# Local attention, channel mix and gated convolution on one core: six chunks of other widths, nine buffers for raw weights, another order

## The chip, the core and the metric

One Trainium2 chip, of which the program uses one core. TensorE (PE) multiplies, with its weight loads shown apart (PEld); VectorE (DVE), ScalarE (ACT) and GpSimd (POOL) do the rest; SyncE (SP) issues transfers. The metric is the time of one execution on the device in microseconds, the median of several runs.

## What is computed

Three steps on float32 data of 4 batches, 576 tokens and 512 channels (8 heads of 64), cut to what matters:

```python
# 1. attention in a window of +-3 tokens, plus attention on means of 4 tokens, repeated 4 times
q_d, k_d, v_d = (t.reshape(B, H, S // 4, 4, D).mean(axis=3) for t in (q, k, v))
out_up = np.repeat(sm_attn(q_d, k_d, v_d), 4, axis=2)
scores = np.where(np.abs(pos[:, None] - pos[None, :]) < 4, scale * q @ k.T, -1e9)
x = out_up + softmax(scores) @ v
# 2. channel mix
xk = mu_k * x + (1 - mu_k) * x_prev;  xr = mu_r * x + (1 - mu_r) * x_prev
v2 = np.maximum(xk @ w_k, 0.0) ** 2 @ w_v            # w_k 512 x 1024, w_v 1024 x 512
x1 = sigmoid(xr @ w_r) * v2                          # w_r 512 x 512
# 3. gated convolution over tokens
h = np.maximum(x1 @ w_in, 0.0)                       # w_in 512 x 1024
conv = sum(conv_w[k] * shifted(h, k - 1) for k in range(3))
out = (h * sigmoid(conv)) @ w_out                    # w_out 1024 x 512
```

## The kernel before

The program is recorded as steps. Each names an engine, a function that emits instructions, and the keys that it reads and writes. `Program.emit` emits the steps by a table of numbers, ORDER, written out in the file; a second table, SECOND, picks the second engine for steps that may run on either of two (`L435`/`L437`: a cast on ScalarE or VectorE). Each engine then works through its own instructions in that order, SyncE's queue of transfers too.

**Precision.** Weights arrive as 8-byte words (`st_d`, 128 partitions of 512 pairs, 512 KB a tile) and become float32 by two ScalarE instructions (`top` L396 into `st_f`, `cut` L415 in place) and one on VectorE (`bits` L399). For most products each operand is split into a high and a low part: a copy (`L435` or `L437`) and a subtraction (`L441`), and three matmuls (high x high, low x high, high x low) stand for one.

**Attention** (`group`, one group of four heads in a batch at a time): `pooled_kq` sums queries and keys by four on VectorE (L526); `local_scores` (L555 mask, L564) and `down_scores` (L629) are matmuls of 32 or 64 rows, followed by maxima, exponentials and normalisations on VectorE (L580 to L602, L646 to L673) and ScalarE (L593, L656, L671); `down_out` and `local_out` transpose the probabilities (L703, L759), copy them out of PSUM on ScalarE (L709, L764), and multiply by v (L727, L805). In batch 0 the means of v come from a matmul (`fold`, L499), and the first six of 18 query blocks are done by themselves, first.

**Channel mix**: `mix_prep` (L880, L888) builds xk for a chunk of tokens. The chunks are 192, 384 and four times 432 tokens. The first (`first_mix`, L919 and L949) multiplies by the raw float32 weights as they arrive, tile by tile (8 of w_k, 8 of w_v), while the tiles are being split for later. The others (`mix`) do 8 up products of 12 matmuls (L983), relu and square and split (L1002 to L1022, into the ring `k2` of 9 slots), and 4 down products of 24 (L1033). Attention of the following batches is placed between them. `out_of_mix` stores v2 to DRAM, `store_x` stores x.

**Last stage**: for five chunks of 384, 512, 512, 512 and 384 tokens, `load_chunk` reads x and v2 back, `gate` multiplies by w_r (L1324), `hidden` by w_in (L1372) with the convolution on VectorE (L1429 to L1442), and `outp` by w_out (L1467).

**What the change touches.** `floats` takes raw words from a ring of three tiles `st_d`: a load can be issued only when L399 has read the tile of three loads ago; until the first mix is done there are four tiles `st_f`. In memory, `first` holds what only the start needs; `mid` holds xk, k2 and the split w_r after it; `low` holds v2 of the last stage. `fills` (L1089) are 20 matmuls without use that stand between steps of the start. The factors mu are loaded by a transfer of their own (L1062) and completed by L1065.

Of the kernel before, what the change touches and what calls it, by code (L numbers as in the profile page):

```python
# [1569 lines left out]
```

## Time and profile before

| | |
|---|---|
| median of 3 runs | 556.81 us (555.5 to 561.09) |
| profiled execution | 556.9 us, its span 554.8 us |
| PE busy | 538.7 us, 97% of the span, 5364 matmuls |
| VectorE busy | 366.3 us, 66% |
| ScalarE busy | 300.3 us, 54% |
| GpSimd busy | 43.5 us, 8% |
| moved by DMA | 66.14 MB, mean 119 GB/s |
| chain that ended last | PE 91%, DMA 3%, DVE 3%, ACT 1%, issue 1% |

The span is counted from the first to the last instruction of the profiled execution. A share of busy time is a mean over stages: the first 77 us (attention of batch 0, the first chunk, the weights) are another kind of work than what follows.

### The profile page before, as it was taken

The numbers are of one execution on the slowest core, as the hardware profiler recorded it, in microseconds if no ns is written. First come the engines' busy times: TensorE is split into PE (matmuls) and PEld (weight loads), VectorE is DVE, ScalarE is ACT, GpSimd is POOL, SyncE is SP. The second block draws the span as 40 slices with busy tenths as digits, with TensorE's granted clock in tenths as the row PEclk, the third lists the DMA queues.
The fourth block names the chain that finished last, engine by engine and source line by source line (L and its number), as shares of the span: only waits on it lengthen the run. The fifth ranks groups of instructions, "written<-read, shape, count | busy, mean of one in ns | idle before, by whom it ended". The sixth has DMA issues, their size and how long they took to land.

```text
span 554.8 us, 12885 instructions
## 1 busy us (share of the span) xinstructions
PE 538.7 (97%) x5364; PEld 479.4 (86%) x5364; DVE 366.3 (66%) x689; ACT 300.3 (54%) x676; POOL 43.5 (8%) x181
## 2 busy tenths in 40 slices
PE   6899899999999999999999999999999999999996
PEld 3788789899898999999999998888888888899985
DVE  4699897675675385456366698579747867766750
ACT  2888676356556555464566646455535443442441
POOL 5001010110101000000000001002001101100000
PEclk9999999999999999999999999999999999999999
DMA  8577883477364614413616022232022000010021
GB/s 325 209 249 205 331 252 104 125 236 223 91 207 126 193 60 142 143 57 129 223 38 222 34 76 77 76 115 95 1 64 107 19 1 2 0 58 21 0 77 57
DMA packets 25402, 66.14 MB, mean 119 GB/s; under 512 B 2688, under 2 KB 8320, under 8 KB 24320
## 3 DMA queue, kind: packets, MB, share of 16 engines
q1 hardware_dynamic: 23616, 62.37, 32.5%
q0 software_dynamic: 1728, 2.95, 3.2%
q8 instruction: 42, 0.69, 0.5%
q14 instruction: 16, 0.13, 0.1%
HBM read 51.15 MB, written 14.16 MB: 118 GB/s over the span
## 4 chain that ended last, share of the span: by engine, by line
PE 91%; DMA 3%; DVE 3%; ACT 1%; issue 1%; SPq 0%; ACTq 0%; DVEq 0%
PE a L1467 18%; PE mm L983 17%; PE mm L1033 17%; PE mm L1372 9%; PE a L1372 9%; PE mm L1324 4%; PE a L1324 4%; PE a L805 3%; PE mm L919 2%; DMA st_d<-in_moe_w_v 2%; DMA vw<-in_vw 2%; PE a L703 1%; PE a L727 1%; PE a L564 1%; PE a L759 1%; PE a L629 1%
## 5 line engine op out<-in xcount | busy, mean ns | idle before, releaser
L983 PE MATMUL mm<-xk,wk 128*128 128x432 f32 (+1 forms) x480 | 97.0, 357 | 0.8 <-issue 0.8
L1033 PE MATMUL mm<-k,wv 128*128 128x432 f32 (+1 forms) x480 | 95.6, 356 | 0.0
L1033 PEld LDWEIGHTS mm<-k,wv 128*128 128x128 f32 x480 | 88.3, 188 | 3.9 <-issue 0.7
L983 PEld LDWEIGHTS mm<-xk,wk 128*128 128x128 f32 x480 | 88.0, 188 | 4.1 <-issue 1.1
L1467 PE MATMUL a<-wk,wv 128*128 128x512 f32 x342 | 81.0, 389 | 0.0
L1467 PEld LDWEIGHTS a<-wk,wv 128*128 128x128 f32 x342 | 64.2, 188 | 13.3
L1372 PE MATMUL mm<-k,wi 128*128 128x512 f32 (+2 forms) x240 | 52.0, 368 | 0.0
L1372 PE MATMUL a<-k,wi 128*128 128x512 f32 (+2 forms) x240 | 51.9, 368 | 0.0
L1372 PEld LDWEIGHTS mm<-k,wi 128*128 128x128 f32 x240 | 44.0, 188 | 5.8
L1372 PEld LDWEIGHTS a<-k,wi 128*128 128x128 f32 x240 | 43.9, 188 | 5.6
L1439 ACT ACTIVATE tmp<-tmp 128x513 f32<-128x513 f32 (+1 forms) x40 | 23.6, 592 | 36.3 <-DVE tmp L1433 36.1
L1002 ACT ACTIVATE tmp<-mm 128x432 f32<-128x432 f32 (+1 forms) x40 | 20.8, 522 | 26.1 <-PE mm L983 11.8
L399 DVE SCALAR_TENSOR_TENSOR st_f<-st_f,st_d 128x512 uint32<-128x512 uint32 x28 | 19.3, 689 | 23.1 <-ACT st_d L415 23.1
L1442 DVE SCALAR_TENSOR_TENSOR tmp<-tmp,h 128x384 f32<-128x384 f32 (+3 forms) x64 | 26.9, 456 | 7.2 <-ACT tmp L1439 5.8
L1022 DVE TENSOR_TENSOR k<-tmp,k 128x432 fp32r<-128x432 f32 (+1 forms) x40 | 23.5, 595 | 9.9 <-ACT k L1014 8.8
L1433 DVE SCALAR_TENSOR_TENSOR tmp<-h,cw_sb,tmp 128x513 f32<-128x513 f32 (+1 forms) x40 | 28.0, 700 | 1.8
L1430 DVE SCALAR_TENSOR_TENSOR tmp<-h,cw_sb,tmp 128x513 f32<-128x513 f32 (+1 forms) x40 | 28.0, 700 | 1.8
L1453 DVE TENSOR_TENSOR wv<-tmp,wv 128x512 fp32r<-128x512 f32 (+1 forms) x32 | 20.0, 628 | 11.6 <-ACT wv L1451 11.4
L391 POOL DMA_DIRECT2D vd<-in_vp x18 | 14.7, 817 | 162.1 <-DMA vd<-in_vp 96.9
L1429 DVE TENSOR_SCALAR tmp<-h,cw_sb 128x513 f32<-128x513 f32 (+1 forms) x40 | 18.4, 460 | 12.2 <-ACT h L1409 11.3
L1482 ACT ACTIVATE st_d<-a 128x512 f32<-128x512 f32 x18 | 10.5, 595 | 27.4 <-PE a L1467 23.7
L1451 ACT CAST wv<-tmp 128x512 fp32r<-128x512 f32 (+1 forms) x32 | 17.9, 571 | 11.8 <-DVE tmp L1442 11.6
(174 smaller groups left out, 874.8 us busy)
## 6 DMA issues: line engine op xcount, KB each, us to landing
vw<-in_vw SPq DMA_DIRECT2D x7, 1152.0 KB, 6.5
kq<-in_kq SPq DMA_DIRECT2D x6, 1152.0 KB, 6.4
x_d<-xT SPq DMA_DIRECT2D x16, 288.0 KB, 3.4
out_dram<-st_d SPq DMA_DIRECT2D x18, 256.0 KB, 2.1
st_d<-in_moe_w_k SPq DMA_DIRECT2D x8, 512.0 KB, 4.3
...
```

The source lines that it names most:

```text
L983: nc.tensor.matmul(pst[:, 0:n], lhsT=wk_t[wt][:, kt, mt * P:(mt + 1) * P], rhs=late["xk"][:, xs, kt, 0:n], start=(kt == 0 and g == 0), sto ...
L1002: lambda r=r, pst=pst: nc.scalar.activation(r, pst[:, 0:n], AF.Relu), (), [pk, rk],
L1022: lambda e, r=r, j=j: e.tensor_sub(late["k2"][1][:, j, 0:n], r, late["k2"][0][:, j, 0:n].bitcast(F32)),
L1033: nc.tensor.matmul(pst[:, 0:n], lhsT=wv_t[wt][:, kt, mt * P:(mt + 1) * P], rhs=late["k2"][xs][:, at[kt], 0:n], start=(kt == 0 and g == 0), ...
L1324: nc.tensor.matmul(pst[:, 0:n], lhsT=late["wr"][wt][:, kt, mt * P:(mt + 1) * P], rhs=r_t(c, xs, kt)[:, 0:n], start=(kt == 0 and g == 0), s ...
L1372: nc.tensor.matmul(pst[:, 0:n], lhsT=late["wi"][wt][:, kt, mt * P:(mt + 1) * P], rhs=x1s(xs, kt)[:, 0:n], start=(kt == 0 and g == 0), stop ...
L1430: nc.vector.scalar_tensor_tensor(out=cv, in0=tap(0), scalar=cw[:, 0, mt:mt + 1], in1=cv, op0=ALU.mult, op1=ALU.add)
L1433: nc.vector.scalar_tensor_tensor(out=cv, in0=tap(2), scalar=cw[:, 2, mt:mt + 1], in1=cv, op0=ALU.mult, op1=ALU.add)
L1439: step("ACT", act(m), lambda: nc.scalar.activation(cv, cv, AF.Tanh, scale=0.5), (), [cvk])
L1442: nc.vector.scalar_tensor_tensor(out=gf[:, o:q], in0=cv[:, o + j:q + j], scalar=1.0, in1=tap(1)[:, o + j:q + j], op0=ALU.add, op1=ALU.mult,)
L1453: ("DVE",), (dve(m),), lambda e: e.tensor_sub(gh_t(1, j)[:, 0:m], gf, gh_t(0, j)[:, 0:m].bitcast(F32)),
L1467: nc.tensor.matmul(pst, lhsT=xs[:, tt * P:(tt + 1) * P], rhs=wo[wt][:, kt, :], start=(kt == 0 and g == 0), stop=(kt == KF - 1 and g == 2),)
```

## The change

- The chunks of the channel mix are 192, 384, 512, 512, 384 and 320 tokens in place of 192, 384 and four of 432. `tmp` and xk grow to 512 columns, `k2` has 8 slots in place of 9.
- Six more tiles of raw words, `st_dd`, lie in `first`: the first nine weight tiles go to nine buffers, later ones to the three of before. The four `st_f` are used by the first twelve.
- The factors mu stand behind v's words in the rows of the first load of v (16 words more); a copy takes them from there. The load of mu is gone.
- Copies from PSUM in batch 0's attention, and the scaling of the first chunk's input, may run on VectorE or ScalarE. `copy` and `any_step` are new.
- The split w_r moves out of `mid` to a pool of its own that takes the place of `sq`; v2 of the last stage lies in `tmp`, one of two tiles of the convolution in the last pool.
- ORDER and SECOND are new tables.

```diff
 ORDER = [
-    4, 3, 79, 8, 9, 5, 10, 201, 0, 81, 69, 13, 70, 66, 2, 61, 62, 80, 15, 16, 97, 23, 17, 89, 24, 25, 63, 26,
+    3, 4, 9, 8, 5, 10, 96, 0, 80, 65, 14, 78, 66, 68, 1, 104, 15, 16, 200, 2, 17, 22, 18, 64, 63, 88, 23, 69,
...
-    NT = 3 * S // 4
+    NT = 4 * P
     ROW = -(-NT // 64) * 64
-    chunks_ = [(0, NH), (NH, S - NH)] + [(t, NT) for t in range(S, B * S, NT)]
-    K2 = 9
+    sizes = [NH, S - NH, NT, NT, 3 * P]
+    sizes.append(B * S - sum(sizes))
+    chunks_ = [(sum(sizes[:i]), n) for i, n in enumerate(sizes)]
+    K2 = 8
...
-    vw_t = several(att, 1, [P, NB // 2, 4, D], F32, "vw") + several(first, 1, [P, NB // 2, 4, D], F32, "vw_f")
+    VW = NB // 2 * 4 * D
+    vw_m = att.tile([P, VW + 16], F32, name="vw")
+    vw_t = [vw_m[:, 0:VW].rearrange("p (e h d) -> p e h d", h=4, d=D)] + several(first, 1, [P, NB // 2, 4, D], F32, "vw_f")
...
+    st_d += several(first, 6, [P, 512, 2], U32, "st_dd")
...
-    def ring(name, tiles, one=0):
+    def ring(name, tiles, one=0, until=None):
         i = count[name] = count.get(name, -1) + 1
-        i %= one or len(tiles)
+        i %= one if until is not None and i >= until else len(tiles) if until is not None else one or len(tiles)
         return tiles[i], (name, i)
...
-        d, dk = ring("st_d", st_d)
+        d, dk = ring("st_d", st_d, 3, 9)
...
-        f, fk = ring("st_f", st_f, 2 * bool(late))
+        f, fk = ring("st_f", st_f, 2, 12)
...
+        def copy(eng, o, i):
+            if eng is nc.vector:
+                eng.tensor_copy(o, i)
+            else:
+                nc.scalar.copy(o, i)
+
+        def any_step(n, f, r, w, slack):
+            if b == 0:
+                step(("ACT", "DVE"), (act(n), 0.12 + 1.0e-3 * n), f, r, w, slack=slack)
+            else:
+                step("ACT", act(n), lambda: f(nc.scalar), r, w, slack=slack)
...
-            load(t.rearrange("p e h d -> p (e h d)"), vw[b, gp], NB // 2 * 4 * D, (), [k], SL[0])
+            if b == 0 and gp == 0:
+                load(vw_m, vw[b, gp], VW + 16, (), [k, "mus0"], SL[0])
+            else:
+                load(t.rearrange("p e h d -> p (e h d)"), vw[b, gp, :, 0:VW], VW, (), [k], SL[0])
...
-                def cp(a=a, e=e, pst=pst):
-                    nc.scalar.copy(pt[:, a:e].rearrange("p i r -> p (i r)"), pst[:, 0:(e - a) * P])
-                step("ACT", act((e - a) * P), cp, (), pks + [(ptk, a)], slack=SL[i0 > 0])
+                def cp(eng, a=a, e=e, pst=pst):
+                    copy(eng, pt[:, a:e].rearrange("p i r -> p (i r)"), pst[:, 0:(e - a) * P])
+                any_step((e - a) * P, cp, (), pks + [(ptk, a)], SL[i0 > 0])
...
-    step("SP", 0.2, lambda: nc.sync.dma_start(out=mus[:, 0:2], in_=mu), (), ["mus0"])
-    step(
-        "DVE", 0.17,
-        lambda: nc.vector.tensor_scalar(mus[:, 2:4], mus[:, 0:2], -1.0, 1.0, op0=ALU.mult, op1=ALU.add),
-        ["mus0"], ["mus"],
-    )
+    def factors():
+        nc.vector.tensor_copy(mus[:, 0:2].rearrange("p a k -> p (a k)"), vw_m[:, VW:VW + 2 * KM])
+        nc.vector.tensor_scalar(mus[:, 2:4], mus[:, 0:2], -1.0, 1.0, op0=ALU.mult, op1=ALU.add)
+
+    step("DVE", 0.28, factors, ["mus0"], ["mus"])
...
-        late["wr"] = several(mid, 2, [P, KM, DM], F32R, "wr")
...
+    def open_wr():
+        sq_pool.release()
+        late["wrp"] = wrp = tc.alloc_tile_pool(name="wrp", bufs=1, reuse_waits="tile")
+        late["wr"] = several(wrp, 2, [P, KM, DM], F32R, "wr")
...
     def v_t(i, kt):
-        return cutout(st_d[1 + kt // 2], kt % 2 * CH, CH, F32) if i else late["v"][0][:, kt]
+        return cutout(st_d[1 + kt // 2], kt % 2 * CH, CH, F32) if i else tmp[:, kt]
...
+    def cv_t(i):
+        return cutout(tmp, KM * NT + 2 * CH, CH + 1, F32) if i else late["cv"][0]
```

Two places of the new order. The first is SyncE's queue, from the second group's queries and keys on. `kq` and `vw` are queries with keys, and v's rows; `kq_f` and `vw_f` those of the second group; `st_d` and `st_dd` are tiles of raw weight words. Before:

```order
L383 DMA kq_f_127<-in_kq 128x768 x2
L383 DMA vw_130<-in_vw 128x2304
L383 DMA vw_f_131<-in_vw 128x2304
L409 DMA st_d_110<-in_moe_w_k 128x1024
L1062 DMA mus<-in_mu 128x8
L383 DMA kq_f_127<-in_kq 128x2x384
L409 DMA st_d_112<-in_moe_w_k 128x1024
L409 DMA st_d_111<-in_moe_w_k 128x1024
L409 DMA st_d_110<-in_moe_w_k 128x1024
L409 DMA st_d_111<-in_moe_w_k 128x1024
```

Now, from the same load on:

```order
L389 DMA kq_f_127<-in_kq 128x768 x2
L389 DMA vw<-in_vw 128x2320
L389 DMA vw_f_131<-in_vw 128x2304
L415 DMA st_d_112<-in_moe_w_k 128x1024
L415 DMA st_d_110<-in_moe_w_k 128x1024
L389 DMA kq_126<-in_kq 128x2x384
L415 DMA st_dd_148<-in_moe_w_k 128x1024
L415 DMA st_d_111<-in_moe_w_k 128x1024
L415 DMA st_dd_150<-in_moe_w_k 128x1024
L389 DMA kq_f_127<-in_kq 128x2x384
L415 DMA st_d_110<-in_moe_w_v 128x1024
L415 DMA st_dd_151<-in_moe_w_k 128x1024
```

The rest of the first group's queries and keys (`kq_126`, 384 columns of two pairs), which stood ahead of these rows, now stands behind two tiles of w_k; five tiles of w_k go out ahead of the first load that reuses a tile (`st_d_110` for w_v), where it was three; the load of mu is gone.

The second place is VectorE's work from the first raw weights to the first channel-mix matmul's inputs. `st_f`, `st_ff` are float32 tiles of w_k, `wk_115` and `wk_116` their high and low parts, `tmp<-xT,mus` the mixed input, one row for each of four tiles of 128 channels. Before:

```order
L399 SCALAR_TENSOR_TENSOR st_f_113<-st_f_113,st_d_110 128x512
L399 SCALAR_TENSOR_TENSOR st_f_114<-st_f_114,st_d_111 128x512
L437 CAST wk_115<-st_f_114 128x4x128
L441 TENSOR_TENSOR wk_116<-st_f_114,wk_115 128x4x128
L888 SCALAR_TENSOR_TENSOR tmp<-xT_119,mus,tmp 128x192
L399 SCALAR_TENSOR_TENSOR st_ff_146<-st_ff_146,st_d_112 128x512
L888 SCALAR_TENSOR_TENSOR tmp<-xT_119,mus,tmp 128x192
L441 TENSOR_TENSOR wk_116<-st_f_113,wk_115 128x4x128
L888 SCALAR_TENSOR_TENSOR tmp<-xT_119,mus,tmp 128x192 x2
```

Now:

```order
L901 TENSOR_SCALAR tmp<-xT_119,mus 128x192
L916 SCALAR_TENSOR_TENSOR tmp<-xT_119,mus,tmp 128x192
L443 CAST wk_115<-st_ff_146 128x4x128
L405 SCALAR_TENSOR_TENSOR st_f_113<-st_f_113,st_d_110 128x512
L447 TENSOR_TENSOR wk_116<-st_ff_146,wk_115 128x4x128
L443 CAST wk_115<-st_f_113 128x4x128
L916 SCALAR_TENSOR_TENSOR tmp<-xT_119,mus,tmp 128x192 x2
L405 SCALAR_TENSOR_TENSOR st_ff_147<-st_ff_147,st_dd_148 128x512
L447 TENSOR_TENSOR wk_116<-st_f_113,wk_115 128x4x128
L916 SCALAR_TENSOR_TENSOR tmp<-xT_119,mus,tmp 128x192
```

One tile's bits (`st_ff_146`) stand just ahead of these rows. The first input's scaling has come over from ScalarE (L901), a second cast too, and the third tile's bits stand between the last two inputs.

## Rows read from the trace of the kernel before

**Rows 1.** The page's head and its first part: busy us, share of span, instructions.

```profile
span 554.8 us, 12885 instructions
PE 538.7 (97%) x5364; PEld 479.4 (86%) x5364; DVE 366.3 (66%) x689; ACT 300.3 (54%) x676; POOL 43.5 (8%) x181
```

**Rows 2.** Busy time by stage; the first row names the columns.

```profile
core 0: us, PE busy (x) PEld busy (x) DVE busy (x) ACT busy (x) POOL busy (x), PEclk, DMA share, GB/s
0.00:4.85 4.85, 0.86 (x4) 0.59 (x5) 0.06 (x1) 2.34 (x5) 3.74 (x20) 1.00 0.61 202
4.85:20.80 15.95, 14.66 (x311) 9.35 (x310) 10.84 (x30) 6.19 (x20) 4.48 (x22) 1.00 0.86 335
18.00:23.00 5.00, 4.66 (x157) 4.34 (x155) 2.18 (x6) 4.26 (x11) 0.00 (x0) 1.00 0.17 49
20.80:28.40 7.60, 6.13 (x242) 5.17 (x239) 4.97 (x12) 7.18 (x16) 0.00 (x0) 0.89 0.49 157
28.40:77.80 49.40, 45.21 (x1059) 40.73 (x1060) 45.37 (x93) 39.07 (x99) 4.17 (x5) 0.98 0.78 258
77.80:131.00 53.20, 52.40 (x870) 48.77 (x869) 36.92 (x70) 31.74 (x85) 5.65 (x7) 1.00 0.61 185
131.00:304.00 173.00, 173.00 (x1736) 162.38 (x1736) 98.32 (x185) 96.41 (x210) 5.55 (x15) 1.00 0.42 136
304.00:551.00 247.00, 246.46 (x1153) 212.37 (x1151) 169.80 (x304) 116.69 (x240) 19.94 (x113) 1.00 0.15 49
```

**Rows 3.** The chain that ended last, in order of time: start us, us, what.

```profile
3.15 8.67 DMA vw<-in_vw
...
59.06 9.62 DMA st_d<-in_moe_w_v
...
77.03 3.34 PE mm L983 x18
...
100.99 2.08 PE mm L1033 x12
...
210.12 18.80 PE mm L1033 x96
...
389.41 21.76 PE a L1467 x96
```

**Rows 4.** SyncE's waits, 0 to 80 us: total us, times, longest.

```profile
SPq L409 <- DVE st_f L399: 22.7, 8, 5.6
SPq L409 <- DVE st_ff L399: 13.8, 6, 4.7
```

**Rows 5.** Waits of PE (4 to 30 us), VectorE and ScalarE (28.4 to 77.8 us).

```profile
PE mm L499 <- DMA vw<-in_vw: 1.3, 1, 1.3
...
DVE st_ff L399 <- ACT st_d L415: 1.0, 1, 1.0
DVE kqd L526 <- DMA kq<-in_kq: 0.8, 1, 0.8
DVE st_f L399 <- ACT st_d L415: 0.5, 2, 0.3
...
ACT st_ff L396 <- DMA st_d<-in_moe_w_v: 2.3, 2, 1.6
...
ACT st_f L396 <- DMA st_d<-in_moe_w_v: 0.9, 1, 0.9
```

**Rows 6.** Groups by line and form: xcount, busy us, mean ns, idle before.

```profile
L581 DVE TENSOR_TENSOR probs<-a,sums 128x684 f32<-128x684 f32 x6 | 5.2, 871 | 0.2
L673 DVE TENSOR_TENSOR pd<-pd,sums 128x720 f32<-128x720 f32 x4 | 3.6, 904 | 0.1
L437 DVE CAST wk<-st_f 128x512 fp32r<-128x512 f32 x5 | 2.1, 423 | 0.1
L888 DVE SCALAR_TENSOR_TENSOR tmp<-xT,mus,tmp 128x192 f32<-128x192 f32 x4 | 1.6, 413 | 0.0
L824 DVE COPY xT<-a 128x192 f32<-128x192 f32 x2 | 0.7, 359 | 1.3 <-PE a L805 1.3
...
L671 ACT ACTIVATE pd<-pd,sums 128x144 f32<-128x144 f32 x13 | 4.3, 406 | 2.7 <-DVE sums L536 2.6
```

**Rows 7.** Instructions in order of time, VectorE and PE: start us, us, what.

```profile
27.73 0.74 DVE L888 SCALAR_TENSOR_TENSOR tmp<-xT,mus,tmp 128x192 f32<-128x192 f32 x2
28.25 2.52 PE L919 MATMUL mm<-tmp,st_f 128*128 128x192 f32 x8
...
34.97 1.50 PE L919 MATMUL mm<-tmp,st_ff 128*128 128x192 f32 x8
```

More of the change, by code (lines that the diff above doesn't have):

```diff
@@ L380, in tile_local_attention__then__channel_mix__then__conv_glu, with load @@
     step("POOL", 4.7, make_picks, (), ["picks"])
-    def load(o, i, words, r, w, slack=1.0, rows=P):
-        step("SP", dma_us(words, rows), lambda: nc.sync.dma_start(out=o, in_=i), r, w, slack=slack)
+    def load(o, i, words, r, w, slack=1.0, rows=P, k=1.0):
+        step("SP", k * dma_us(words, rows), lambda: nc.sync.dma_start(out=o, in_=i), r, w, slack=slack)
     def load_sum(o, planes, words, keys, slack, rows=P):
@@ L471, in loads @@
                     len(prs) * (e - a), (),
-                    [(k, i, pr) for pr in prs for i in ({0, half} if whole else {i0})], SL[i0 > 0],
+                    [(k, i, pr) for pr in prs for i in ({0, half} if whole else {i0})], SL[i0 > 0], P, 1.0,
                 )
@@ L736, in down_out, with cp @@
             whole = m // BQ * BQ
-            def cp():
-                nc.scalar.copy(od[:, :, 0:whole], po[:, :, 0:whole])
+            def cp(eng):
+                copy(eng, od[:, :, 0:whole], po[:, :, 0:whole])
                 if m > whole:
-                    nc.scalar.copy(od[:, :, whole:m], po[:, :, nq * BQ - (m - whole):nq * BQ])
-            step("ACT", act(2 * whole), cp, (), pks + [odk], slack=SL[i0 > 0])
+                    copy(eng, od[:, :, whole:m], po[:, :, nq * BQ - (m - whole):nq * BQ])
+            any_step(2 * whole, cp, (), pks + [odk], SL[i0 > 0])
         def local_out(i0, i1):
@@ L1110, in open_mid @@
         late["k2"] = several(mid, 2, [P, K2, ROW], F32R, "k2")
-        late["wr"] = several(mid, 2, [P, KM, DM], F32R, "wr")
-    seconds = [("st_f", 2), ("st_f", 3)] + [(x, 1) for x in ("kq", "kqd", "vw", "vd", "probs", "pd")]
+    seconds = [("st_f", 2), ("st_f", 3)] + [("st_d", 3 + i) for i in range(6)] + [(x, 1) for x in ("kq", "kqd", "vw", "vd", "probs", "pd")]
     step("", 0.0, open_mid, (), [k for k in prog.writer if root(k, seconds)] + ["mid"])
     late["two"] = True
-    by_columns(w_r, lambda: late["wr"][0], lambda: late["wr"][1], KM, range(KM), "wr", ["mid"])
+    def open_wr():
+        sq_pool.release()
+        late["wrp"] = wrp = tc.alloc_tile_pool(name="wrp", bufs=1, reuse_waits="tile")
+        late["wr"] = several(wrp, 2, [P, KM, DM], F32R, "wr")
+    step("", 0.0, open_wr, ["mid"], [k for k in prog.writer if root(k) == "sq"] + ["wrp"])
+    by_columns(w_r, lambda: late["wr"][0], lambda: late["wr"][1], KM, range(KM), "wr", ["wrp"])
     store_x(0)
@@ L1139, in tile_local_attention__then__channel_mix__then__conv_glu @@
     att_keys = [k for k in prog.writer if root(k) in names]
-    sq_keys = [k for k in prog.writer if root(k) == "sq"]
     def open_late():
-        sq_pool.release()
         att.release()
-        late["low"] = low = tc.alloc_tile_pool(name="low", bufs=1, reuse_waits="tile")
-        late["v"] = several(low, 1, [P, KM, CH], F32, "v")
         wb = late["pool"] = tc.alloc_tile_pool(name="wb", bufs=1, side="right", reuse_waits="tile")
@@ L1151, in open_late @@
         late["edge"] = several(wb, 1, [P, KF, ahead + 1], F32, "edge")
-        wb.tile([P, 72], F32, name="gap2")
-    step("", 0.0, open_late, (), att_keys + sq_keys + ["late"])
+        late["cv"] = several(wb, 1, [P, CH + 1], F32, "cv")
+        wb.tile([P, 192], F32, name="gap2")
+    step("", 0.0, open_late, ["wrp"], att_keys + ["late"])
     class Late:
@@ L1219, in v_dst @@
             return [(2 * j, 2 * j + 2, flat(st_d[1 + j], F32).rearrange("p (k c) -> p k c", k=2)) for j in range(2)]
-        return [(0, KM, late["v"][0])]
-    v_old = ("late", "st_old")
+        return [(0, KM, tmp[:, 0:KM])]
+    v_old = ("tmp_lo", "st_old")
     xrf = [cutout(xT[1], CH * i, CH, F32) for i in range(2)]
@@ L1225, in tile_local_attention__then__channel_mix__then__conv_glu @@
     os_t = [cutout(st_d[0], DM * i, DM, F32) for i in range(2)]
-    cv_t = [cutout(tmp, (CH + 1) * i, CH + 1, F32) for i in range(2)]
-    gt_t = [cutout(tmp, 2 * (CH + 1) + CH * i, CH, F32) for i in range(2)]
+    gt_t = [cutout(tmp, KM * NT + CH * i, CH, F32) for i in range(2)]
+    def cv_t(i):
+        return cutout(tmp, KM * NT + 2 * CH, CH + 1, F32) if i else late["cv"][0]
     GB = 10
@@ L1239, in tile_local_attention__then__channel_mix__then__conv_glu @@
     step("", 0.0, lambda: None, (), keys_of("k2") + ["k2_old"])
+    step("", 0.0, lambda: None, (), [k for k in prog.writer if k[0] == "tmp" and k[1] < KM] + ["tmp_lo"])
     step("", 0.0, lambda: None, (), keys_of("tmp") + ["tmp_old"])
@@ L1423, in hidden @@
         parts = [0] + [t - outs[c][0] for t in seam] + [m]
-        cv, cvk = ring("cv", cv_t)
+        ci, cvk = ring("cv", (0, 1))
         gt, gk = ring("gt", gt_t)
-        cv, gf = cv[:, 0:m + gap], gt[:, 0:m]
+        gf = gt[:, 0:m]
         def conv():
+            cv = cv_t(ci)[:, 0:m + gap]
             nc.vector.tensor_scalar_mul(cv, tap(1), cw[:, 1, mt:mt + 1])
@@ L1437, in hidden, with tanh @@
         hks = [(hk, "pad"), (hk, "d")]
-        step("DVE", 0.43 + 3.36e-3 * m, conv, hks + ["cw", "tmp_old"], [cvk])
-        step("ACT", act(m), lambda: nc.scalar.activation(cv, cv, AF.Tanh, scale=0.5), (), [cvk])
+        step("DVE", 0.43 + 3.36e-3 * m, conv, hks + ["cw", "tmp_old", "late"], [cvk])
+        def tanh():
+            cv = cv_t(ci)[:, 0:m + gap]
+            nc.scalar.activation(cv, cv, AF.Tanh, scale=0.5)
+        step("ACT", act(m), tanh, (), [cvk])
         def glu():
+            cv = cv_t(ci)
             for j, (o, q) in enumerate(zip(parts, parts[1:])):
@@ L1508, in tile_local_attention__then__channel_mix__then__conv_glu @@
     late["pool"].release()
-    late["low"].release()
+    late["wrp"].release()
     late["mid"].release()
@@ L1514 @@
 _INS = [
[L1515 removed]
+    "kq", "vp", "vw", "moe_w_k", "moe_w_v", "moe_w_r",
     "moe2_w_in", "moe2_conv_w", "moe2_w_out",
@@ L1546 @@
     laid["vp"] = vd.transpose(0, 1, 5, 6, 2, 4, 3, 7).reshape(B, H // 4, 80, FAC, -1)
-    laid["mu"] = np.stack([inputs[x].reshape(-1, P).T for x in ("moe_mu_k", "moe_mu_r")], axis=1)
+    mu = np.stack([inputs[x].reshape(-1, P).T for x in ("moe_mu_k", "moe_mu_r")], axis=1).reshape(P, -1)
+    vw = laid["vw"]
+    laid["vw"] = np.zeros((*vw.shape[:3], vw.shape[3] + 16), vw.dtype)
+    laid["vw"][..., :vw.shape[3]] = vw
+    laid["vw"][0, 0, :, vw.shape[3]:vw.shape[3] + mu.shape[1]] = mu
     laid["moe2_conv_w"] = inputs["moe2_conv_w"].reshape(3, -1, P).transpose(2, 0, 1).reshape(P, -1)
```

42 lines of the change are left out of this document (22 added, 20 removed), and 165 rows, old and new, of tables (ORDER, SECOND).

## The prediction

> **What bounds the kernel now.** I read the engines' busy times first. TensorE is busy for 538.7 of 554.8 us [rows 1], so only about 16 us of the span are without a matmul, and the other two ways to win time are cheaper matmuls and fewer fillers. The table by stage [rows 2] then shows where the 16 us lie. From 131 us to the end PE shows no gap but the store at the very end: 173.00 of 173.00 and 246.46 of 247.00. Between 77.8 and 131 it misses 0.8 us. The rest, 3.99 + 1.29 + 1.47 + 4.19 = 10.9 us, lies ahead of 77.8 us. In the columns beside them, the stretch from 28.4 to 77.8 has VectorE at 45.37 of 49.40 us; ScalarE has 39.07. So the kernel has two parts: a start of 77 us in which VectorE (and ScalarE close behind) feeds PE, and 477 us in which only the cost of the matmuls counts.
>
> The chain of waits, in order of time [rows 3], says the same. Ahead of 77 us it passes through transfers (v's rows to 11.8 us, a tile of w_v from 59.06 to 68.68 us) and then VectorE; behind that it is blocks of matmuls back to back. The sync engine's waits [rows 4] tell why the tile of w_v was late: its queue stood for 22.7 and 13.8 us at loads of raw weights, until VectorE's L399 had emptied one of three buffers. DMA meanwhile moved 49 GB/s from 18 to 23 us, against 335 GB/s in the stretch ahead [rows 2].
>
> **The change, part by part.** All sums are against the profiled execution, 554.8 us of span; its time was 556.9 us, so 2.1 us lie around the span, and the median of the runs shown (556.81) is the same time.
>
> *Chunks.* The number of chunks stays six, so the number of matmuls stays (192 in each chunk with split operands, 96 up and 96 down), and the columns sum to the same 2304. Only the price of a column changes. Blocks without a gap give it [rows 3]: 96 of 432 columns take 18.80 us, 195.8 ns each; 96 of 512 columns 21.76 us, 226.7 ns; 12 of 384 columns 2.08 us, 173.3 ns. Over 1/2.4 ns a column that is 15.8, 13.3 and 13.3 ns a matmul. A width of 320 does not occur. With the surplus of 384 and 512 it is 146.7 ns, with that of 432 it is 149.2; I take 146.7, since a line drawn through 384 and 512 down to 320 gives it too. Before: 4 x 192 x 195.8 = 150.4 us. After: 192 x (226.7 + 226.7 + 173.3 + 146.7) = 148.5 us. That is **-1.9 us**, or -1.4 at the other end. It falls in the part where PE has no gap, so all of it reaches the end, as long as what feeds PE keeps up: from 131 to 304 us VectorE is busy for 98.32 and ScalarE for 96.41 of 173 us [rows 2], so a block of 12 shorter by 0.6 us (146.7 against 195.8 ns) still leaves them room, and two blocks of down products stand between the last square of a chunk and the block that needs it.
>
> Against this speaks a rule of the Trainium skill, page "TensorE: Matmul & The Clock Gate", section "Wait — 56ns, not 53.3ns?": back to back, a warm matmul starts N / 2.4 GHz plus a fixed 2.5 ns after the one ahead of it. By that rule equal columns in equally many matmuls cost the same, and the sum would lack the 1.9 us. The trace does not agree with it: 15.8 ns at 432 and 13.3 ns at 512 columns [rows 3].
>
> *Nine raw-word buffers.* Six more tiles let the first nine loads of weights go without L399 having emptied one. In SP's order five loads of w_k now stand ahead of the first that must wait (before, three). The price of the waits that go: ScalarE stood 2.3 + 0.9 us for tiles of w_v, and VectorE 1.0 us behind that, and 0.8 us for queries and keys queued at SP behind such loads [rows 5]. VectorE bounds the stretch. Its idle time there is 49.4 - 45.4 = 4.0 us, its whole list of named waits 3.2 us. I count 1.0 + 0.8 + 0.5 (the two short waits for the cut of raw words) = **-2.3 us**; the bounds are 0 (another wait takes the place) and -4.0 (VectorE never stands).
>
> *Work that moves between VectorE and ScalarE.* Some evacuations of PSUM in batch 0 and the first scaling may now run on VectorE. By the order on both engines, from the start to the last piece of the first split chunk VectorE gets 138 instructions in place of 131: eleven come, four go. Nine of the new ones are copies from PSUM of 256 to 768 columns, which VectorE does not do in this trace. I price them along the line through its copy of 192 columns (359 ns) and its subtraction from PSUM of 684 (871 ns) [rows 6]: 0.43 us for each of five with 256, 0.56 for 384, 0.69 for each of two with 512, 0.96 for 768, in all 5.05 us. The scaling (at most 0.41, as L888 on 192 columns) and the copy of the factors (8 words, below 0.2) make it 5.6. What goes: two copies of 192 (0.72), a normalisation of 720 columns (0.904), a cast (0.423). Net +3.6 us. But it comes early: ahead of the first matmul of the channel mix VectorE is idle for 15.95 - 10.84 + 7.60 - 4.97 = 7.7 us [rows 2], which covers the 4.0 us that fall there. Behind it, in the stretch that counts, VectorE gets the copies of 768 and one of 256 columns and loses the normalisation and two casts: 0.96 + 0.43 - 0.90 - 0.85 = -0.4 us. I leave that at **0**, since ScalarE takes the normalisation in five pieces of 0.406 us [rows 6], though it has 49.40 - 39.07 = 10 us of room there. If the early cover were gone, the 4.0 us would be on the path.
>
> *Order at the start.* SP's second load is now the other half-batch's, and the rest of the first queries and keys (384 columns of two pairs, 0.39 MB, 1.2 us at 335 GB/s) comes behind v's rows. The first fold of v waited 1.3 us for those rows [rows 5], which landed at 3.15 + 8.67 = 11.82 us [rows 3]; it can start up to 1.2 us earlier. What follows is attention of the first six blocks on PE, VectorE and ScalarE in turn, up to L399 and L888, whose last piece ended at 27.73 + 0.74 = 28.47 us [rows 7]. That last piece stands behind three tiles' bits, as before, and now behind one cast more; so I take **-0.5 us** of the 1.2, bounds +1 and -1.2.
>
> *The rest.* The factors ride in v's rows: one small load fewer, one tiny copy more on VectorE (0.1 us, early): 0. Twenty fillers stay twenty. PE's granted clock is at 0.89 from 20.8 to 28.4 and at 0.98 from 28.4 to 77.8 us [rows 2], a stretch at 1.2 GHz after small waits around 25 us; the first channel-mix matmuls still wait for the same work, so I leave it as it is. The k2 ring of eight serves eight products: its slots 0 to 3 are read for the last time a block before the chunk's last. Where v, cv and the gate's tiles lie in the last stage adds no instruction; VectorE has 247 - 170 us of room there: 0, as is the new order of blocks. Switches between attention and mix number 29 in place of 28.
>
> **Sum**: 554.8 - 1.9 - 2.3 - 0.5 = 550.1 us of span, 552.2 us with the 2.1 around it.
>
> **Rivals.**
> 1. *VectorE never stands.* Its idle 4.0 us vanish, the start gains all 1.2 us, and the 0.8 us behind 77.8 too: 554.8 - 1.9 - 4.0 - 1.2 - 0.8 = 546.9, 549.0 us in all. For it: no load of raw words is on the path any more. Against: ScalarE has 2 us more there, and each tile passes ScalarE, VectorE, PE in turn.
> 2. *The buffers bring nothing.* VectorE was at 92% there; its waits for transfers turn into waits for ScalarE. Only the columns are left: 552.9, 555.0 us in all. For it: 45 us of VectorE's work stay.
> 3. *The width isn't it.* The 432's surplus comes from the stage's operands, not its width, and chunks of 512 pay it too, or all pay one floor: 550.1 + 1.9 = 552.0, 554.1 us in all. Against: L1033 at 384 columns, same operands, has 13.3 ns. The rule of the Trainium skill named above gives this time. The trace bears it out in nothing but the equal surplus of 384 and 512.
> 4. *Slower.* The copies given to VectorE come in its full stretch and not in the idle one ahead: the place is its queue between the folds of v and the first bits, the price 4.0 us, less the columns' 1.9: 556.9, 559.0 us in all. It decides once the first channel-mix matmul starts 2 us behind 28.25 us. Beyond it a second stretch at 1.2 GHz at the start would cost about what the first did (a block of 8 in 2.52 in place of 1.50 us [rows 7]).
>
> **How the numbers follow.** Forecast 0.52, rival 1 0.22, rival 2 0.14, rival 3 0.04, rival 4 0.08. The predicted time is the forecast's, 552.2 us. The range leaves out rival 4 (0.08) and the half of rival 1 that lies below its time (0.11): 549.0 to 556.0 us, which holds the ends of the column and buffer terms too. A measurement can tell about 1% from no change: faster is below 551.2, slower above 562.4. Faster: rival 1 and a sixth of the forecast, 0.31; slower: what of rival 4 reaches past 562.4, and the unseen, 0.07; same: the rest, 0.62.
>
> **What would show it.** Right: blocks of 96 in 21.76 us (512) and about 14.1 us (320); SP's waits at L399's successor much shorter until 50 us; no wait of ScalarE for w_v; the first product of 384 columns at about 74 us in place of 77.03; PE without gaps from 131 us on. Wrong: VectorE busy over 95% and the 384s no earlier (rival 2); 512 at more than 228 ns (rival 3); the first channel-mix matmul behind 30 us (rival 4); gaps on PE in the chunk of 320 columns or at the first gates.

## The result, and the profile after

The changed kernel takes 552.02 us (median of ten runs, 551.51 to 552.67), the kernel before beside it 556.62 us (ten runs, 555.31 to 561.09): a ratio of 0.990, interval 0.988 to 0.993. Run once more with the last experiments it took 551.84 us. So it is faster by 4.6 us, close to the forecast of 552.2 us; that is 0.8%, less than the 1% from which the prediction counted a change. The parts of the forecast fared less evenly than its sum.

The page's head and first part, to be read beside [rows 1]:

```profile
span 550.3 us, 12876 instructions
PE 537.8 (98%) x5364; PEld 469.2 (85%) x5364; DVE 376.6 (68%) x711; ACT 290.7 (53%) x655; POOL 47.0 (9%) x181
```

The number of matmuls is the same, TensorE's busy time fell by 0.9 us only, and the span by 4.5. Busy time by stage, with the columns of [rows 2]; the fourth row runs from the last piece of the first mix input to the first product of 384 columns:

```profile
4.85:20.80 15.95, 14.97 (x314) 9.85 (x312) 11.36 (x33) 4.99 (x16) 4.38 (x24) 1.00 0.99 391
18.00:23.00 5.00, 4.15 (x116) 3.71 (x110) 2.38 (x6) 1.59 (x4) 0.00 (x0) 0.91 0.64 249
20.80:28.40 7.60, 7.16 (x241) 6.09 (x238) 6.05 (x14) 4.90 (x12) 0.00 (x0) 0.59 0.20 60
29.14:74.83 45.69, 43.85 (x1056) 38.70 (x1054) 44.10 (x89) 39.88 (x104) 4.17 (x5) 1.00 0.70 229
131.00:299.47 168.47, 168.47 (x1804) 149.86 (x1803) 99.25 (x189) 86.29 (x190) 5.54 (x15) 1.00 0.41 129
```

The stretch of the fourth row in the kernel before:

```profile
28.47:77.03 48.56, 44.37 (x1055) 39.89 (x1055) 44.60 (x91) 38.96 (x99) 4.17 (x5) 0.98 0.77 257
```

VectorE's work in it hardly changed (44.60, then 44.10 us), but it stands for 45.69 - 44.10 = 1.6 us in place of 48.56 - 44.60 = 4.0 us. Ahead of it TensorE's granted clock is 0.59 from 20.8 to 28.4 us, where it was 0.89 [rows 2]. Where each stage begins, from the timeline of VectorE and TensorE (start us, us, what):

```profile
28.74 0.40 DVE L916 SCALAR_TENSOR_TENSOR tmp<-xT,mus,tmp 128x192 f32<-128x192 f32 x1
...
74.83 6.63 PE L1011 MATMUL mm<-xk,wk 128*128 128x384 f32 x36
...
125.05 1.31 PE L1011 MATMUL mm<-xk,wk 128*128 128x512 f32 x5
...
299.31 0.87 PE L1353 MATMUL mm<-xk,wr 128*128 128x386 f32 x4
```

With the same four places before (28.47, 76.95, 128.77 and 303.95 us by its timeline) the 4.5 us are:

| stretch | before | after | difference |
|---|---|---|---|
| to the last piece of the first mix input | 28.47 | 29.14 | +0.7 |
| from there to the first product of 384 columns | 48.48 | 45.69 | -2.8 |
| the chunk of 384 | 51.82 | 50.22 | -1.6 |
| the four wide chunks | 175.18 | 174.26 | -0.9 |
| last stage | 250.9 | 251.0 | +0.1 |

The chunk of 384 and the wide chunks share attention work: the new order puts 80 fewer local score matmuls, with 4 masks, into the chunk of 384 (by the matmuls' start times this work takes 1.97 us there in place of 3.05) and as many more behind it. Without that shift of about 1.1 us the chunk of 384 gained about 0.5 us and the wide chunks about 2.0 us. In a second profile of the changed kernel (span 549.5 us, the last of the experiments) the four places are at 29.17, 75.09, 124.07 and 298.36 us: the chunk of 384 takes 48.97 us there, 1.3 less than in the table, and the other stretches differ by 0.3 at most.

The 0.7 us to the last piece were lost ahead of ScalarE's and VectorE's work for it. By the chain these two take 7.4 us to that piece in both kernels, from the first of the next rows before and from the second now (start us, us, what):

```profile
21.08 0.58 ACT pdt L709
```

```profile
21.73 0.03 ACT xT L841
```

TensorE's wait for v's rows at the first fold (1.3 us before) is gone from the list of waits all the same. Which step of the attention ahead of 21.7 us became longer was not tested.

SyncE's waits to 80 us and the named waits of VectorE (28 to 76 us) and TensorE (74 to 300 us), beside [rows 4, 5]:

```profile
SPq L415 <- DVE st_f L405: 21.7, 3, 11.0
SPq L389 <- PE a L746: 11.7, 2, 6.4
SPq L415 <- DVE st_ff L405: 8.1, 2, 5.3
...
DVE pt L468 <- PE a L778: 0.6, 1, 0.6
DVE sums L556 <- ACT pd L677: 0.2, 1, 0.2
...
PE a L746 <- DMA vd<-in_vp: 0.9, 1, 0.9
```

SyncE's queue still stands for 21.7 + 8.1 us at loads of raw words, in five waits where there were fourteen; but nobody waits for w_v any more, and VectorE's named waits fell from 3.2 to 0.8 us. TensorE's wait of 0.9 us at 86.15 us is new.

### The profile page after: what moved, and what is told of

Same layout as the page of the kernel before. It is cut to its first block, busy times and chain, and to the rows that moved or that the text cites. A ratio compares the mean times of both kernels' runs of the same rounds, so it can differ in the third digit from the quotient of the medians.

```text
span 550.3 us, 12876 instructions
## 1 busy us (share of the span) xinstructions
PE 537.8 (98%) x5364; PEld 469.2 (85%) x5364; DVE 376.6 (68%) x711; ACT 290.7 (53%) x655; POOL 47.0 (9%) x181
## 4 chain that ended last, share of the span: by engine, by line
PE 90%; DMA 4%; DVE 2%; POOL 1%; ACT 1%; issue 1%; ACTq 0%; POOLq 0%
PE a L1504 18%; PE mm L1061 17%; PE mm L1011 15%; PE mm L1401 9%; PE a L1401 9%; PE mm L1353 5%; PE a L1353 4%; DMA vd<-in_vp 4%; PE a L824 3%; PE mm L947 2%; PE a L746 2%; PE a L724 1%; PE mm L977 1%; PE a L585 1%; PE a L778 1%; PE a L650 1%
## 5 line engine op out<-in xcount | busy, mean ns | idle before, releaser
L1061 PE MATMUL mm<-k,wv 128*128 128x384 f32 (+2 forms) x480 | 95.6, 355 | 0.0
L1011 PE MATMUL mm<-xk,wk 128*128 128x384 f32 (+2 forms) x480 | 95.5, 355 | 0.0
L1030 ACT ACTIVATE tmp<-mm 128x384 f32<-128x384 f32 (+2 forms) x40 | 20.8, 524 | 36.6 <-PE mm L1011 32.0
L1037 DVE TENSOR_TENSOR tmp<-tmp 128x512 f32<-128x512 f32 (+2 forms) x28 | 16.4, 591 | 24.0 <-ACT tmp L1030 24.0
L397 POOL DMA_DIRECT2D vd<-in_vp x18 | 14.7, 815 | 163.8 <-DMA vd<-in_vp 130.9
L1050 DVE TENSOR_TENSOR k<-tmp,k 128x384 fp32r<-128x384 f32 (+2 forms) x40 | 23.2, 592 | 7.9 <-ACT k L1042 7.2
L1353 PE MATMUL mm<-xk,wr 128*128 128x512 f32 (+2 forms) x120 | 26.1, 369 | 0.0
L1353 PE MATMUL a<-xk,wr 128*128 128x512 f32 (+2 forms) x120 | 25.9, 368 | 0.0
L1353 PEld LDWEIGHTS a<-xk,wr 128*128 128x128 f32 x120 | 22.0, 188 | 2.8
L1353 PEld LDWEIGHTS mm<-xk,wr 128*128 128x128 f32 x120 | 21.9, 188 | 2.8
L1504 PE MATMUL a<-wk,k 128*128 128x512 f32 x90 | 22.9, 390 | 0.0
```

What stands on the lines that cost most here:

```text
L397: lambda i=i: nc.gpsimd.dma_start(out=o, in_=i, accum_op=ALU.add), (), keys, slack=slack,
L1011: nc.tensor.matmul(pst[:, 0:n], lhsT=wk_t[wt][:, kt, mt * P:(mt + 1) * P], rhs=late["xk"][:, xs, kt, 0:n], start=(kt == 0 and g == 0), sto ...
L1030: lambda r=r, pst=pst: nc.scalar.activation(r, pst[:, 0:n], AF.Relu), (), [pk, rk],
L1037: e.tensor_tensor(out=r, in0=r, in1=r, op=ALU.mult)
L1050: lambda e, r=r, j=j: e.tensor_sub(late["k2"][1][:, j, 0:n], r, late["k2"][0][:, j, 0:n].bitcast(F32)),
L1061: nc.tensor.matmul(pst[:, 0:n], lhsT=wv_t[wt][:, kt, mt * P:(mt + 1) * P], rhs=late["k2"][xs][:, at[kt], 0:n], start=(kt == 0 and g == 0), ...
```

## The experiments

### The chunks' widths alone

```diff
-    sizes = [NH, S - NH, NT, NT, 3 * P]
-    sizes.append(B * S - sum(sizes))
+    sizes = [NH, S - NH] + [3 * S // 4] * 4
```

> The changed kernel with its four wide chunks set back to 432 columns each, rows of tiles still 512 words apart, and the order of steps, the buffers and the engines of the changed kernel. Theory A (steady prices of 195.8 against 226.7, 173.3 and 146.7 ns): 1.9 us more than the changed kernel, 553.9 us. Theory A2 (the same prices, but a chunk of 512 columns gives some of it back each time it follows attention work, since its first six or so matmuls take 228 to 236 ns): 1.1 us more, 553.1 us. Rival B (the width isn't it): 552.0 us, blocks of 96 at 432 columns below 18.6 us or the gain of the middle stretch unchanged.

Measured: 553.52 us (552.71 to 556.41, eight runs), 1.5 us above the changed kernel and 1.7 above its second run. On every engine the instructions stand in the same order in both, so this is the price of the widths. The chain of waits of this kernel, then of the changed one (start us, us, what):

```profile
244.57 18.80 PE mm L1060 x96
263.37 18.80 PE mm L1010 x96
```

```profile
226.90 11.11 PE mm L1061 x48
238.01 16.66 PE mm L1011 x96
254.67 16.64 PE mm L1061 x96
271.31 14.07 PE mm L1011 x96
```

A matmul costs 195.8 ns at 432 columns, 173.5 at 384 and 146.6 at 320. No block of 96 at 512 columns is free of attention work. In the 48 from 226.90 us the start times in the trace are 338 ns apart for the first, 228 to 236 for the next five, and from then on 226, 227 and 227 in turn: 226.7, as in the last stage. At 432 columns the spacing never settles, it runs through 189, 192, 197, 198, 198, 202, 198 and 193 ns over and over. Each kernel enters mix blocks from attention work 19 times in these chunks, in the changed kernel always at 512 columns. From start to start, the 768 wide matmuls take 153.18 us at 432 columns (0.28 of it a wait) and 151.51 us in the changed kernel: 1.7 us. The steady prices give 1.9 us, the wait adds 0.3, and each entry costs about 25 ns more at 512 than at 432 columns, 19 x 25 ns = 0.5 us the other way.

### The buffers alone

In the kernel before, nothing else changed:

```diff
-        d, dk = ring("st_d", st_d)
+        d, dk = ring("st_d", st_d, 3, 9)
...
+    st_d += several(first, 6, [P, 512, 2], U32, "st_dd")
```

> The kernel before with nine raw-word buffers for the first nine loads and nothing else: its order, its chunks of 432 columns, its engines for the copies. Theory A (the buffers take VectorE's waits away, whatever the order): 2.3 us less than before, 554.3 us (bounds 552.6 and 556.6), the first product of 384 columns at about 74.8 us in place of 77.03, VectorE's idle time between 28.4 and 77 us down from 4.0 to about 1.7 us. Rival B (buffers alone bring nothing, the new order of steps does): 556.6 us, 384s at 77 us, VectorE's named waits replaced by waits for ScalarE.

Measured: 556.6 us, ratio to before 1.001 (0.999 to 1.003): nothing. The first product of 384 columns is at 77.07 us. Two things cancel. Between the last piece of the first mix input and that product VectorE stands for 47.77 - 44.72 = 3.05 us, 0.9 less than before. But that piece ends at 29.38 us, 0.9 later. This kernel's row for that stretch, then TensorE's timeline ahead of that piece, and ScalarE's waits (28.4 to 78 us), which show what stayed:

```profile
29.38:77.15 47.77, 44.30 (x1055) 39.90 (x1055) 44.72 (x91) 39.05 (x100) 4.23 (x5) 0.98 0.74 249
```

```profile
21.44 1.13 PE L787 MATMUL a<-pdt,vd_f 80*64 80x64 f32 x32 [0.34 <-ACT pdt L710]
23.71 0.50 PE L787 MATMUL a<-pdt,vd_f 80*64 80x64 f32 x9 [1.14 <-issue]
```

```profile
ACT st_ff L397 <- DMA st_d<-in_moe_w_v: 2.0, 2, 1.1
```

TensorE stands for 1.14 us in the middle of a line with nothing to wait for, and its clock falls to 1.2 GHz right behind that (mean 0.62 from 23 to 28.4 us, against 0.85); that this made the piece late is likely, but no run tests it alone. ScalarE's wait for w_v stays (2.0 us here, 2.3 before): those tiles are among the last four of sixteen loads, which still share three buffers. VectorE's wait for queries stays as well (0.9 us here, 0.8 before).

### The buffers and w_v's loads moved up

The run above, with SyncE's seven loads of w_v that reuse a buffer put right behind the step that empties it; the first of them, in SyncE's order:

```diff
 DMA st_d<-in_moe_w_k 128x1024
+DMA st_d<-in_moe_w_v 128x1024
 DMA st_dd<-in_moe_w_k 128x1024
+DMA st_d<-in_moe_w_v 128x1024
 DMA st_dd<-in_moe_w_k 128x1024
```

> The kernel before with nine raw-word buffers, as in the run with the buffers alone (556.6 us), and besides with the seven loads of w_v that reuse a buffer moved up in the sync engine's queue to right behind the step that empties it; nothing else moves on any engine. Theory A (with the buffers alone those loads stand behind loads of queries and v that wait for TensorE, and the early loads of w_k fill the transfer engines just when TensorE's program stands for 1.1 us at 22.6 us; the order of the loads mends both): 1.5 to 3 us less than the run with buffers alone, 553.6 to 555.1 us, the first product of 384 columns at 74.5 to 76 us, no wait of ScalarE for w_v above 0.5 us. Rival B (the gain needs the new order of the work on TensorE, VectorE and ScalarE too): 556 to 557 us.

Measured: 558.05 us (556.31 to 560.07), ratio 1.001 (0.999 to 1.004), the first product of 384 columns at 76.91 us: rival B. The idle 1.1 us at 22.6 us are gone, and so are transfers there (DMA busy for 0.21 of 18 to 23 us, 0.79 in the run above). Idle time of the same kind came back where transfers now run: 0.91 us ahead of 27.30 us and 1.00 us ahead of 81.30 us. So this load order with the old order of work gains nothing in sum. Again two things cancel: the last piece of the first mix input ends at 30.32 us, 1.9 later than before, behind a wait of ScalarE for a tile of w_k (2.0 us) and one of VectorE for ScalarE (1.7 us); the stretch behind it takes 46.6 us, 1.9 less than before, though ScalarE still waits 0.8 us for a tile of w_v (columns of [rows 2]):

```profile
30.32:76.91 46.59, 43.92 (x1052) 39.19 (x1051) 44.50 (x91) 38.95 (x100) 4.16 (x5) 0.97 0.71 236
```

### The new order with three buffers, or with the old loads

The first takes the six extra tiles out of the changed kernel; a load whose buffer is not free yet comes behind the step that frees it (and on ScalarE two pairs of the instructions that make such a tile float32 come later with it):

```diff
-        d, dk = ring("st_d", st_d, 3, 9)
+        d, dk = ring("st_d", st_d[:3])
```

> The changed kernel with three raw-word buffers in place of nine; where its order asks for a load ahead of the step that empties the buffer, the load comes right behind that step, and all else keeps its order. Theory A (buffers): the sync engine stands again, 1.5 to 4 us more than the changed kernel, 553.5 to 556 us, the first product of 384 columns at 76.3 to 78.8 us in place of 74.8, ScalarE or VectorE waiting for raw words again. Rival B (the order and the copies carry the gain): within 0.7 us of 552.0 us.

Measured: 562.15 us (562.06 to 562.5), ratio to before 1.009 (1.007 to 1.012): ten us above the changed kernel, far outside what either theory gave. The first product of 384 columns is at 86.30 us. SyncE's waits, 0 to 80 us, and ScalarE's for raw words (28 to 80 us):

```profile
SPq L430 <- DVE st_ff L420: 22.5, 6, 7.8
SPq L430 <- DMA st_d<-in_moe_w_k: 15.3, 3, 8.7
SPq L430 <- DVE st_f L420: 13.8, 6, 4.6
...
ACT st_ff L417 <- DMA st_d<-in_moe_w_k: 4.1, 1, 4.1
ACT st_f L417 <- DMA st_d<-in_moe_w_v: 4.1, 1, 4.1
```

The second keeps nine buffers and the order on TensorE, VectorE, ScalarE and GpSimd word for word, and puts only SyncE's early loads back into the old order:

```diff
 DMA kq<-in_kq 128x768 x2
+DMA kq<-in_kq 128x2x384
 DMA kq_f<-in_kq 128x768 x2
 ...
-DMA st_d<-in_moe_w_v 128x1024
 DMA st_dd<-in_moe_w_k 128x1024
-DMA st_d<-in_moe_w_v 128x1024
 ...
 DMA kq<-in_kq 128x2x1152
```

> The changed kernel with the loads of its first part issued by the sync engine in the order of the kernel before (the rest of queries and keys ahead of v's rows, w_v's tiles behind the loads of queries and pooled v); nothing moves on TensorE, VectorE, ScalarE or GpSimd. Theory A (the new order of the work gains only with loads in its own order, the buffers alone do not let the old load order do): 1 to 6 us more than the changed kernel, 553 to 558 us, ScalarE or VectorE waiting for raw words or queries again. Rival B (the order of the work on the engines gains by itself, whatever the order of loads): within 0.5 us of 552.0 us, first product of 384 columns at 74.5 to 76 us.

Measured: 559.53 us (557.23 to 563.63), ratio 1.005 (1.003 to 1.008), 7.7 us above the changed kernel run beside it; the first product of 384 columns is at 81.03 us. SyncE's waits (0 to 80 us), then those of ScalarE and VectorE (28 us on):

```profile
SPq L386 <- PE a L743: 12.4, 2, 8.8
SPq L386 <- DVE kqd L544: 12.4, 1, 12.4
SPq L412 <- DVE st_ff L402: 12.1, 2, 8.6
...
ACT st_f L399 <- DMA st_d<-in_moe_w_v: 3.0, 1, 3.0
...
DVE pt L465 <- PE a L775: 3.3, 1, 3.3
DVE st_ff L402 <- ACT st_dd L418: 2.0, 1, 2.0
```

Loads of w_v stand behind loads of queries and of v, which wait for TensorE and VectorE to free their tiles; ScalarE then waits for w_v, VectorE for ScalarE and TensorE.

A third kernel took the other half: the kernel before with nine buffers, and the new order for its first 200 steps on four engines.

> The kernel before with nine raw-word buffers, as in the run with the buffers alone (556.6 us, first product of 384 columns at 77.07 us), with the first 200 of some 1590 steps, up to the last tiles of w_k, in the order of the changed kernel on the sync engine, TensorE, VectorE and ScalarE; the engines of the copies, the 432 columns and all later steps as before. Theory A (the gain of the start is that the new order uses the loads that the buffers let run ahead, and lies ahead of about 50 us): 1 to 2.5 us less than with the buffers alone, 554.1 to 555.6 us, first product of 384 columns at 75 to 76 us. Rival B (it lies in the order of the w_v tiles behind 50 us or in the engines of the copies): 556 to 557 us, 384s at about 77 us.

Measured: 567.07 us (563.72 to 568.89). It says nothing between its two theories. Orders that do not belong together cost 10 us once more, here against the buffers alone: SyncE stood for 32.7 us at L397 and VectorE for 7.5 us at queries.

### The copies back on ScalarE

```diff
-                step(("ACT", "DVE"), (act(n), 0.12 + 1.0e-3 * n), f, r, w, slack=slack)
+                step("ACT", act(n), lambda: f(nc.scalar), r, w, slack=slack)
```

and likewise for the copies of the folded v and the first scaling.

> The changed kernel with the first batch's copies out of PSUM, the copies of the folded values and the first scaling all on ScalarE, as they stood before. Theory A (the copies on VectorE are covered by its early idle time, and ScalarE has room): within 0.7 us of 552.0 us. Theory B (the copies stand in VectorE's full stretch): faster by up to 4 us, 548 us. Theory C (ScalarE is late at the start, which the moved copies mend): 1 to 2 us more, 553 to 554 us, the last piece of the first mix input later than 29.1 us.

Measured: 552.51 us (eight of twelve runs between 552.15 and 552.62, the other four from 553.3 to 557.69), 0.5 us above the changed kernel: theory A. Its profiled execution took 556.4 us, an untypical one, so no row of it is used.

### What bounds the changed kernel's start

Two kernels take away what the profile points at: VectorE's work, and the small waits ahead of the low clock.

```diff
-SECOND = {..., 154, ..., 162, 168, ...}      # three casts of w_v on VectorE
+SECOND = {...}                               # on ScalarE
```

> The changed kernel with three casts of w_v tiles (0.42 us each on VectorE, about 0.61 us each on ScalarE) moved to ScalarE, between 55 and 70 us. Theory A (VectorE, which is idle for 1.5 of 46 us ahead of 75 us, bounds the stretch alone): 0.8 to 1.3 us less than the changed kernel, 550.7 to 551.2 us. Rival B (VectorE, ScalarE and TensorE are level there, 5.8, 5.8 and 6.0 of each 6 us between 58 and 64): 0 to 1.5 us more, 552.0 to 553.5 us, with VectorE waiting for ScalarE.

Measured: 552.19 us (552.11 to 552.4): rival B. VectorE has less to do and stands for more (columns of [rows 2], then its waits):

```profile
29.00:76.13 47.13, 44.49 (x1055) 39.04 (x1054) 43.46 (x87) 41.69 (x108) 4.17 (x5) 0.99 0.70 229
```

```profile
DVE sums L556 <- ACT pd L677: 1.0, 1, 1.0
DVE sums L617 <- ACT probs L614: 0.7, 1, 0.7
DVE wv L447 <- ACT wv L441: 0.7, 1, 0.7
```

Its idle time is 3.7 us, more than twice that of the changed kernel, and the first product of 384 columns comes 1.2 us later. So taking work off VectorE and giving it to ScalarE wins nothing: VectorE isn't the bound by itself.

```diff
-            for _ in range(2):
+            for _ in range(2 if k[1] in (0, 1, 2, 7) else 3):
```

with fillers 0 and 1 moved to 19.6 us and 2 and 7 to 21.7 us.

> The changed kernel with four of its ten fillers (two matmuls each) moved to the two places at 19.6 and 21.7 us where TensorE stands ahead of the fall to 1.2 GHz at 22.4 us; the other six are longer by half, so the early work of fillers stays. Theory A (those small waits bring on the stretch at half clock, and it costs): granted clock near 1.0 until 28 us, attention of the first half-batch ends 1 us earlier, and since VectorE is full from 24.7 us on, 0.3 to 1 us less than the changed kernel, 551.0 to 551.7 us. Rival B (VectorE sets the pace whatever the clock): clock up, time within 0.3 us of 552.0. Rival C: the fillers delay what they precede by up to 0.25 us each, clock unchanged: 552.0 to 552.5 us.

Measured: 553.36 us (551.96 to 554.28). The waits are filled (TensorE busy for 5.00 of 5.00 us from 18 to 23 us) and the granted clock from 23 to 28.4 us rises to 0.86, yet the first matmuls of the channel mix start at 28.43 us (28.23 in the changed kernel), the last piece of the first mix input ends at 30.04 us (29.14), and the time is 1.3 us longer. So the higher clock won nothing here. Whether the moved fillers took back what it gave, as in rival C, this run can't tell; but by the changed kernel's chain of waits ScalarE and VectorE alone are on the path from 21.7 to 33.5 us, and TensorE's clock is not.

### The new wait for pooled v

One kernel puts the product that waited for it behind the next block of up products, the other takes transfers away from beside the load (1.6 MB of w_r and x, moved behind the load that waits for that product).

```diff
-..., 338, 335, ..., 341, 336, 497, 383, ...     # 335: the product at 86.15 us
+..., 338, ..., 341, 383, 335, 336, 497, ...     # 383: a block of 12 up products
```

> The changed kernel with the product of pooled probabilities and pooled values that waited 0.9 us at 86.15 us for GpSimd's summing loads put behind the next block of 12 up products, with its copy and the load that follows it. Theory A (that wait lies on the chain): 0.9 us less than the changed kernel, 551.1 us, no wait for vd there. Rival B (something else is late next, such as what the copy feeds): within 0.3 us of 552.0 us, with a new wait of TensorE between 86 and 100 us.

```diff
-..., 253, 317, 258, 313, 263, ..., 274, ..., 275, ..., 336, 497, 383, ...
+..., 253, 317, 313, ..., 336, 497, 258, 263, 274, 275, 383, ...
```

> The changed kernel with two of three loads of w_r and two stores of x (together 1.6 MB) moved in the sync engine's queue to behind the load that waits for the product at 86.15 us, so that they no longer run beside GpSimd's last summing load of pooled values (8.0 us in the changed kernel, 4.3 to 4.6 us for those ahead of it). Theory A (that load sets when the product can start, and the transfers beside it make it slow): it takes 4 to 6 us, TensorE's wait of 0.9 us there goes, 0.5 to 0.9 us less than the changed kernel, 551.1 to 551.5 us. Rival B (VectorE's and ScalarE's work in the 384 chunk is late next): within 0.3 us of 552.0 us. Rival C (the later loads of w_r are late for their bits): slower by up to 1 us.

Measured: the first 553.16 us (552.65 to 553.74), 1.1 us slower. Its wait for pooled v is gone, and TensorE waits 0.7 + 0.6 us for ScalarE's copies instead:

```profile
PE a L775 <- ACT pt L467: 0.7, 1, 0.7
PE a L775 <- ACT od L467: 0.6, 1, 0.6
```

The second took 552.43 us (551.3 to 553.1). Its profile has no wait for pooled v and a span of 549.6 us, which would look like a gain of 0.7 us.

> The changed kernel itself once more, beside the one above on the same chip, to tell how far one number of it can be trusted against the variants: 551.5 to 552.7 us, the first product of 384 columns between 74.8 and 76.1 us as in the variants that leave its start alone.

Measured: 551.84 us, and a profile with a span of 549.5 us that has no such wait either. So the wait stood in one execution of the same kernel and not in another, and moving the transfers gains nothing. In the repeated run the chain of waits is TensorE's from 46.7 us on; from 59.9 us to the first product of 384 columns it is busy for 15.12 of 15.26 us, VectorE for 15.05. The chain's last rows ahead of that product:

```profile
71.63 1.50 PE mm L977 x8
73.12 0.32 PE a L576 x4
73.44 0.43 PE a L585 x31
73.88 0.14 issue
74.02 1.15 PE a L585 x88
75.16 6.46 PE mm L1011 x36
```

No variant beat the changed kernel.

## Why the prediction was right, and where it was not

- **Columns, -1.9 us: right in kind, 0.2 to 0.4 too large.** At the same order the widths are worth 1.5 to 1.7 us. The prices of 384 and 512 columns held, and 320 cost 146.6 ns, as drawn through the other two. What the sum lacked is that a block entered from attention work does not start at its steady price, and that the wider chunk pays more for that. Rival 3 is out: equal columns in equally many matmuls do not cost the same here, which the Trainium skill's rule in "TensorE: Matmul & The Clock Gate", section "Wait — 56ns, not 53.3ns?", would give; the surplus over 1/2.4 ns a column is 13.3 to 13.4 ns at 320 and 512 columns and 15.8 at 432, not 2.5.
- **Nine buffers, -2.3 us: the step that failed.** Alone they brought 0.0 (1.001, interval 0.999 to 1.003), the end of the range that the prediction kept as rival 2. The text priced ScalarE's and VectorE's waits for tiles of w_v as if the first nine loads held them; they belong to the last four of sixteen, and stayed (2.0 us in place of 2.3 at one line, 0.3 in place of 0.9 at the other). So did the 0.8 us for queries. The 0.9 us that VectorE did save was given back ahead of 29.4 us. With w_v's loads moved up as well the stretch itself was 1.9 us shorter, near the priced 2.3, and the start lost as much.
- **Order, -0.5 us: too small, and counted in the wrong place.** Up to the last piece of the first mix input the new order lost 0.7 us, where 0.5 was to be won. Behind it VectorE's idle time fell by 2.4 us, which the text had given to the buffers. The runs show that it takes the three together: against the kernel before, the buffers without the order bring 0, the buffers and w_v's loads moved up 0; against the changed kernel, the order without the buffers costs 10 us, the order and the buffers without its load order 7.7 us. Net, the first product of 384 columns moved by -2.1 us (forecast -2.8), or -1.9 by the second profile. So the sum came out in part by luck: the start fell 0.7 us short, and the chunk of 384, for which the sum had nothing, gave about 0.5; and the start's gain was put down to one part of a set of which no part shortens the time by itself.
- **Moved copies, 0: nearly.** They are worth 0.5 us, not far above the 0.2 by which two series of the changed kernel differ. The line through two widths priced them well: the copies on VectorE take 415 ns at 256 columns, 557 at 384, 683 at 512 and 954 at 768 (0.43, 0.56, 0.69 and 0.96 us in the text), and VectorE's work up to the last piece grew by 3.1 us (15.9 to 19.0) where 4.0 was counted. Rival 4 fell: the first channel-mix matmul is at 28.23 us, and with the copies back on ScalarE the time is not better.
- **The low clock, left as it was: it became longer** (mean 0.59 in place of 0.89 from 20.8 to 28.4 us), and this cost nothing that the run with moved fillers could win back. From 21.7 to 33.5 us the chain does not pass through TensorE.
- **What bounds the start.** "VectorE feeds PE" agrees with the waits before; in the changed kernel VectorE (44.10 of 45.69 us) and TensorE (43.85) are level in that stretch, ScalarE (39.88) is busy enough that VectorE waits for it when it gets three casts more, and 1.3 us taken off VectorE bring nothing. Rival 1, in which VectorE never stands, did not come: it still stands for 1.6 us. Where the chunk of 384 won its 0.5 us (1.7 by the second profile) was not tested apart; before, TensorE stood there for 0.8 us with nothing to wait for.

Of the signs named ahead, four came about as told (320 in 14.07 us for 96, no ScalarE wait for w_v, the first 384 product at 74.83 us for "about 74", no gaps from 131 us on). Two did not: until 50 us SyncE's queue at raw loads still stands for 21.7 us behind L405, where it was 23.3 behind L399, though behind 28 us no engine waits for raw words any more; and there was no free block of 96 at 512 columns to read. Half of rival 2's sign came, VectorE busy for 96.5% of the stretch, but the 384s are earlier.
